# Two units of two neighbouring blocks beside each other in TensorE, 64 rows each, and the second layer's sums by channels

## The chip, the cores and the metric

One core of a Trainium2 chip runs the whole program. The metric is the device time of one execution in microseconds (us), the median of several. The kernel before takes 1239.06 us (median of 3 runs, 1237.01 to 1239.71).

## The reference, cut to what matters

```python
# x: (2, 4096, 192), weight: (8, 7); 8 heads of 24 channels
w = softmax(weight, axis=-1)
y[b, s, h, g] = sum_k w[h, k] * x_pad[b, s + k, h, g]     # causal, 7 taps
y = y.reshape(8192, 192)
h = y @ w_in                                              # 192 -> 2048
g = max(h, clip((h + 1) / 2, 0, 1) ** 2)                  # what the first layer's gate comes to
z = g @ w_out                                             # 2048 -> 192
h = z @ w_in2
out = (s * max(h, 0) ** 2 + b) @ w_out2                   # (8192, 192) float32
```

All inputs and outputs are float32. The second layer's `s` and `b` are scalars, so the kernel takes them out of the sum: out = s * (max(h, 0)^2 @ w_out2) + b * (column sums of w_out2).

## The kernel before, in words

**Tiles.** The 8192 tokens are 16 blocks of 512 (`NB`). The 2048 inner channels are 16 tiles of 128 (`f`). A unit is one layer, one block, one `f`: 512 units. Every product is made of several in a rounded format: an operand is split into a high part and a low part (`hA`, `lA`, `gh`, `gl`), and high x high, high x low and low x high are summed in PSUM.

**A unit.** `p1` (line 926) makes `h`, 128 inner channels by 512 tokens, of five matmuls with 512 columns: three for the first 128 of the 192 input channels (A), two for the last 64 (B). For B the high part of the weights stands in one half of the array's 128 rows, the low part in the other, and the moving tile holds the 64 channels twice, so that one pass makes two of the products. Then ScalarE and VectorE work on `h`: first layer a clip on ScalarE (line 975), a square (982), a maximum with `h` on VectorE (988); second layer a Relu (996) and a square (1003); in both the rounding to `gh` (967) on ScalarE and the rest `gl` (1010) on VectorE. The second product adds into PSUM banks over all 16 `f`. In the first layer it stands by channels: `pA` takes three matmuls (1022 to 1024) and `pB` two (1027, 1028), 512 columns each. In the second layer it stands by tokens: `gh` and `gl` are the weights, and for each of four groups of 128 tokens 384 columns of `w_out2` (high and low part) run against `gh` (1043) and 192 against `gl` (1044).

**After the last `f`.** In the first layer `evac_first` copies `pA` and adds the two halves of `pB` (1070, 1078, 1085). In the second layer `evac_second` scales on ScalarE (1136) and VectorE (1145), adds the bias on GpSimd (1159), and SyncE stores 96 KB for each 128 tokens.

**Banks.** PSUM has eight banks: four for `h` (`NH`), four for sums (`a`). A first-layer block uses two of the four, a second-layer block all four.

**Order.** Six stages: 6 blocks of layer one, 5 of layer two, and so on (`PHASES`); the first two blocks run in turns, unit by unit, and a third joins them. `Plan` is a list scheduler: each operation has a priority, a cost and the engines that it may run on, and the planner writes down one fixed order for each engine. Tiles come from pools ("f" and "o" are 512 columns wide), and an operation waits in the plan until a tile is free. The convolution of blocks 0 to 3 is done with matmuls (lines 845 and 872); that of the others on VectorE (698 to 725), while units of other blocks run. The weights arrive in 17 pieces, each split into high and low parts by five ScalarE and ten VectorE operations or so (544 to 650). At the start, `spread` (line 454) makes 16 small float32 matmuls, each of them two instructions with 32 rows: four products for each of the four groups of 32 rows, every group with a PSUM bank of its own.

## Time and profile before

| | |
|---|---|
| median of 3 runs | 1239.06 us |
| the profiled execution | 1239.57 us |
| its span, first to last instruction | 1237.9 us |
| TensorE matmuls busy | 1222.7 us (99%), 6096 instructions |
| TensorE weight loads busy | 1039.3 us (84%) |
| ScalarE busy | 1011.3 us (82%), 1791 instructions |
| VectorE busy | 757.3 us (61%), 1235 instructions |
| GpSimd busy | 49.6 us (4%), 86 instructions |
| mean granted clock of TensorE | 0.995 |

PE is TensorE's matmul row, PEld its weight loads, which run beside matmuls; DVE is VectorE, ACT ScalarE, POOL GpSimd, SP SyncE. The duration of a matmul in the trace is longer than the time until the next one starts, since matmuls follow each other in a pipeline; rates are read from starts.

### The profile page before, as it was taken

How to read it: one execution, taken by the hardware profiler on the slowest of the kernel's cores; microseconds unless marked ns; L12 is line 12 of the kernel's file. 1: busy time of each engine (PE TensorE's matmuls, PEld its weight loads, DVE VectorE, ACT ScalarE, POOL GpSimd, SP SyncE). 2: the span in 40 equal slices, each digit the busy share in tenths (PEclk: the TensorE clock that was granted, in tenths of full speed). 3: DMA queues.
4: the chain of work that ended last, by engine and by line, in shares of the span. 5: the costliest groups of instructions: out<-in, count | busy, mean ns of one | idle time of the engine just before them, and what ended most of it. 6: DMA issues, size and time to landing. Idle time of an engine off the chain costs nothing.

```text
span 1237.9 us, 16698 instructions
## 1 busy us (share of the span) xinstructions
PE 1222.7 (99%) x6096; PEld 1039.3 (84%) x6096; DVE 757.3 (61%) x1235; ACT 1011.3 (82%) x1791; POOL 49.6 (4%) x86
## 2 busy tenths in 40 slices
PE   7999999999999999999999999999999999999998
PEld 7877777879988987887888988888888888988887
DVE  5998999983333558695753333766875653333432
ACT  5898889987888888787788888887777778888886
POOL 1000000000000100000000000100000000000000
PEclk8999999999999999999999999999999999999999
DMA  5251312210001101100000001010100000000000
GB/s 134 68 111 26 73 31 60 45 26 5 19 22 31 31 14 27 19 18 10 9 9 4 19 22 40 22 34 16 26 1 1 9 9 3 20 22 23 22 14 13
DMA packets 67849, 34.24 MB, mean 28 GB/s; under 512 B 43197, under 2 KB 64183, under 8 KB 67767
## 3 DMA queue, kind: packets, MB, share of 16 engines
q1 hardware_dynamic: 67415, 32.94, 11.4%
q8 instruction: 47, 0.77, 0.3%
q14 instruction: 35, 0.29, 0.1%
q10 hardware_dynamic: 352, 0.25, 0.1%
HBM read 19.53 MB, written 6.29 MB: 21 GB/s over the span
## 4 chain that ended last, share of the span: by engine, by line
PE 82%; DVE 9%; ACT 6%; issue 1%; DMA 1%; POOL 0%; SPq 0%; POOLq 0%; DVEq 0%; ACTq 0%
PE h L926 41%; PE a L1043 16%; PE a L1044 7%; PE a L1024 4%; PE a L1027 3%; PE a L1028 3%; PE a L1023 3%; PE a L1022 3%; DVE o L1010 2%; DVE f L988 2%; DVE f L725 2%; ACT o L967 2%; ACT f L982 1%; ACT f L975 1%; PE h L845 1%
## 5 line engine op out<-in xcount | busy, mean ns | idle before, releaser
L1010 DVE TENSOR_TENSOR o<-f,o 128x512 fp32r<-128x512 f32 x512 | 357.4, 700 | 419.6 <-ACT o L967 417.0
L926 PE MATMUL h<-o,w 128*128 128x512 f32 x1536 | 445.5, 398 | 0.8 <-ACT o L750 0.6
L967 ACT CAST o<-f 128x512 fp32r<-128x512 f32 x509 | 313.9, 619 | 61.7 <-DVE f L988 52.3
L926 PE MATMUL h<-o,wB 128*128 128x512 f32 x1024 | 320.9, 394 | 0.0
L1043 PE MATMUL a<-w,o 128*128 128x384 f32 x1024 | 308.6, 357 | 0.7 <-DVE f L1085 0.7
L926 PEld LDWEIGHTS h<-o,w 128*128 128x128 f32 x1536 | 269.0, 188 | 46.4 <-ACT o L750 0.8
L1044 PE MATMUL a<-w,o 128*128 128x192 f32 x1024 | 257.2, 251 | 0.3 <-DVE o L1010 0.3
L926 PEld LDWEIGHTS h<-o,wB 128*128 128x128 f32 x1024 | 192.3, 188 | 45.7 <-DVE o L790 0.5
L996 ACT ACTIVATE f<-h 128x512 f32<-128x512 f32 x256 | 153.2, 598 | 76.0 <-PE h L926 75.3
L1043 PEld LDWEIGHTS a<-w,o 128*128 128x128 f32 x1024 | 192.2, 188 | 16.9 <-DVE y L1145 4.6
L1044 PEld LDWEIGHTS a<-w,o 128*128 128x128 f32 x1024 | 194.8, 190 | 10.6 <-DVE o L1010 0.5
L975 ACT ACTIVATE f<-h 128x512 f32<-128x512 f32 x256 | 152.0, 594 | 51.0 <-PE h L926 49.5
L988 DVE TENSOR_TENSOR f<-f,h 128x512 f32<-128x512 f32 x256 | 173.0, 682 | 23.0 <-ACT f L982 22.5
L1003 ACT ACTIVATE f<-f 128x512 f32<-128x512 f32 x256 | 161.8, 632 | 8.1
L982 ACT ACTIVATE f<-f 128x512 f32<-128x512 f32 x256 | 162.0, 633 | 4.5
L1024 PE MATMUL a<-o,w 128*128 128x512 f32 x256 | 103.1, 403 | 2.3 <-DVE o L1010 2.1
L1022 PE MATMUL a<-o,w 128*128 128x512 f32 x256 | 102.1, 399 | 0.2 <-ACT o L967 0.2
L1023 PE MATMUL a<-o,w 128*128 128x512 f32 x256 | 101.3, 396 | 0.0
L1027 PE MATMUL a<-o,w 128*128 128x512 f32 x256 | 100.9, 394 | 0.0
L1028 PE MATMUL a<-o,w 128*128 128x512 f32 x256 | 100.9, 394 | 0.0
L1159 POOL TENSOR_TENSOR y<-y,bias 128x192 f32<-128x192 f32 x64 | 44.5, 727 | 1182.7 <-DVE y L1145 881.1
L1024 PEld LDWEIGHTS a<-o,w 128*128 128x128 f32 x256 | 48.2, 188 | 21.4 <-DVE o L1010 10.2
(86 smaller groups left out, 664.0 us busy)
## 6 DMA issues: line engine op xcount, KB each, us to landing
f<-f SPq DMA_DIRECT2D x56, 128.0 KB
out_dram<-y SPq DMA_DIRECT2D x64, 96.0 KB
raw<-in_moe_w_out_dram SPq DMA_DIRECT2D x15, 384.0 KB
f<-in_x_dram SPq DMA_DIRECT2D x66, 68.0 KB
raw<-in_moe_w_in_dram SPq DMA_DIRECT2D x15, 256.0 KB
raw<-in_moe_w_in_dram SPq DMA_DIRECT2D x18, 128.0 KB
x<-in_x_dram SPq DMA_DIRECT2D x13, 120.0 KB
raw<-in_moe_w_out_dram SPq DMA_DIRECT2D x2, 192.0 KB
```

What stands on the lines that cost most here:

```text
L926: nc.tensor.matmul(h.ap, v, m.ap, start=(k == 0), stop=(k == len(terms) - 1))
L967: nc.scalar.copy(gh.ap, R())
L975: lambda _: nc.scalar.activation(R(), h.ap, IDENTITY_SAT15_5, scale=15.5),
L982: lambda _: nc.scalar.activation(R(), R(), AF.Square, bias=0.5, scale=1.0 / 31.0),
L988: lambda _: nc.vector.tensor_tensor(R(), R(), h.ap, op=ALU.max),
L996: lambda _: nc.scalar.activation(R(), h.ap, AF.Relu),
L1003: lambda _: nc.scalar.activation(R(), R(), AF.Square),
L1010: lambda _: nc.vector.tensor_tensor(gl.ap, R(), gh.ap.bitcast(F32), op=ALU.subtract),
L1022: nc.tensor.matmul(pA.ap, cols(P), gh.ap, start=first, stop=False)
L1024: nc.tensor.matmul(pA.ap, cols(P), gl.ap, start=False, stop=last)
L1043: nc.tensor.matmul(to, gh.ap[:, c], v, start=first, stop=False)
L1044: nc.tensor.matmul(to[:, 0], gl.ap[:, c], v[:, 0], start=False, stop=last)
```

## The change

- Two units run in one step: one of an even block and one of the odd block next to it, which is one `f` behind (`LAG`). So one of the two always has an even `f`, the other an odd one.
- The matmuls of a step have 64 rows each. One unit's matmul stands in rows 0 to 63 of the array, the other unit's in rows 64 to 127, each with its own weights, its own moving rows and its own PSUM bank. The B part of `p1` is three matmuls with 64 rows, with no doubled weights; of each matmul over 128 channels every unit does one half of the rows, and the other half later, when the two units have changed sides. `p1` is six pairs of matmuls and then three, the second product five pairs and then five.
- Before a unit adds into its bank from the other half of the rows, the earlier half must be through: `through` has GpSimd clear one element after the last matmul of the first part, and the first matmul of the second part waits for that.
- The first two steps and the last ones still use 128 rows (`full`, `full2`).
- The second layer's second product stands by channels, as in the first layer: `pA` with three terms and `pB` with two, 512 columns. `evac_second` scales and adds the bias by channels, VectorE transposes in 32x32 blocks, and the output is stored in pieces of 32 channels (`put_blocks`); the last two blocks are turned by TensorE and stored in rows (`put_rows`).
- The stages are 6, 4, 4, 6, 6, 6 blocks. The operands of a block are made five steps ahead (`GATE`). There are 26 "o" tiles in place of 19, 11 "f" tiles in place of 16, and the three "x" tiles become six "f" tiles once the first convolutions are done (`heirs`). A weight piece does two ScalarE casts and one VectorE add fewer.

```diff
-NX = 3
-XKEY = ((0, 2), (1.5, 2), (32.2, 1))
-PHASES = (6, 5, 5, 5, 5, 6)
-NRAW, NZ, NW, NFB, NOB, NY, NXW = 2, 1, 1, 16, 19, 4, 3
+PHASES = (6, 4, 4, 6, 6, 6)
+LAG = 1
+GATE = 5
+NFULL = 2
+NRAW, NZ, NW, NFB, NOB, NXW = 2, 1, 1, 11, 26, 3
...
-    units = sorted(
-        ((0, j, f) for j in range(NX) for f in range(NF)),
-        key=lambda t: XKEY[t[1]][0] + XKEY[t[1]][1] * t[2],
...
+    rows = [], []
+    done = [0, 0]
+        for j in range(done[l], done[l] + n):
+            rows[j % 2].extend((l, j, f) for f in range(NF))
...
+    steps = len(rows[0]) + LAG
+    step_of = {t: 2 * (k + LAG * q) + q for q in range(2) for k, t in enumerate(rows[q])}
...
+            pl.op(
+                need - 2.5,
+                dve1(P),
+                lambda _: nc.vector.tensor_tensor(
+                    tB.ap[:, P : 2 * P], wb.ap[:, colB:cols], zb.ap[:, colB:cols], op=ALU.add
+                ),
...
+    def units(k):
+        us = []
+        for q in range(2):
+            n = k - LAG * q
+            if 0 <= n < len(rows[q]):
+                us.append((2 * k + q, *rows[q][n], Buf("h"), Buf("o"), Buf("o")))
+        u0, full = us[0][0], k < NFULL or len(us) < 2
+        full2 = full or k >= len(rows[0]) - 2
+        us.sort(key=lambda t: t[3] % 2)
+        halves = [((UP, DN)[t[3] % 2]) for t in us]
+        hs = [t[4] for t in us]
+        def termsA(t):
+            (_, l, j, f, *_), op = t, operands[t[1], t[2]]
+            i, o = at[l, f]
+            w = lambda c: wF[l, i].ap[:, o, c : c + P]
+            return ((w(0), op["hA"]), (w(0), op["lA"]), (w(LOW), op["hA"]))
+        def termsB(t):
+            (_, l, j, f, *_), op = t, operands[t[1], t[2]]
+            w = wB[l, f // 2].ap
+            return ((w[:, 0:P], op["Bh"]), (w[:, 0:P], op["Bl"]), (w[:, P : 2 * P], op["Bh"]))
...
+        def through(u, bank):
+            def go(_):
+                i = nc.gpsimd.memset(seen.ap, 0.0)
+                tc.add_manual_dep(i.ins, lasts[bank], sync, reason="last of the one half")
+                lasts[bank] = i.ins.name
+            pl.op(u, ("pool", 100.0), go, reads=(bank,), parts=(seen,))
+        def side_by_side(terms, hv, start, stop):
+            follows = not start and lasts.get(hs[-1])
+            for n, ks in enumerate(zip(*terms)):
+                for (w, m), r, h in list(zip(ks, hv, hs))[:: 1 if start else -1]:
+                    i = nc.tensor.matmul(
+                        h.ap,
+                        w[r],
+                        m.ap[r],
+                        start=start and n == 0,
+                        stop=stop and n == len(terms[0]) - 1,
+                    )
+                    if follows:
+                        tc.add_manual_dep(i.ins, follows, sync, reason="first of the other half")
+                        follows = None
+            lasts[h] = i.ins.name
+        kw = dict(reads=[b for t in us for b in reads(t)], writes=hs)
+        if full:
+            def p1(_):
+                for t, h in zip(us, hs):
+                    for n, (w, m) in enumerate(termsA(t)):
+                        nc.tensor.matmul(h.ap, w, m.ap, start=n == 0, stop=False)
+                side_by_side([termsB(t) for t in us], halves, False, True)
+            cost = (3 * len(us) + 3) * SLOT + DRAIN
+            p1_ops.append(pl.op(u0, ("pe", cost), p1, after=p1_ops[-1:], **kw))
+        else:
+            def p1(_):
+                side_by_side([termsB(t) + termsA(t) for t in us], halves, True, False)
+            def p1_rest(_):
+                side_by_side([termsA(t) for t in us], halves[::-1], False, True)
+            p1_ops.append(pl.op(u0, ("pe", 6 * SLOT), p1, after=p1_ops[-1:], **kw))
+            through(u0, hs[1])
+            pl.op(u0 + 0.1, ("pe", 3 * SLOT), p1_rest, **kw)
+        for u, l, j, f, h, gh, gl in us:
+            between(u, l, h, gh, gl)
...
+            i, o = at[l, f]
+            if f == 0:
+                acc[l, j] = Buf("a"), Buf("a")
+            pA, pB = acc[l, j]
+            w = lambda c: wF[l, i].ap[:, o, c : c + P]
+            return (
+                (pA, lambda: w(P), gh, 0),
+                (pA, lambda: w(ROW - P), gh, 1),
+                (pA, lambda: w(P), gl, 2),
+                (pB, lambda: w(2 * P), gh, 0),
+                (pB, lambda: w(2 * P), gl, 2),
+            )
...
+        def p2(e, hv, start, stop):
+            follows = not start and lasts.get(terms[-1][3][0])
+            for n in (0, 1, 2, 3, 4) if start else (3, 4, 0, 1, 2):
+                for ts, (first, last), r in list(zip(terms, ends, hv))[:: 1 if start else -1]:
+                    p, w, m, at_n = ts[n]
+                    i = nc.tensor.matmul(
+                        p.ap,
+                        w()[r],
+                        m.ap[r],
+                        start=first and start and at_n == 0,
+                        stop=last and stop and at_n == 2,
+                    )
+                    if follows:
+                        tc.add_manual_dep(i.ins, follows, sync, reason="first of the other half")
+                        follows = None
+            lasts[p] = i.ins.name
...
+        if full2:
+                u0 + 2.5,
+                ("pe", 5 * len(us) * SLOT),
+                lambda e: p2(e, [slice(0, P)] * len(us), True, True),
...
+        else:
+            hv = (UP, DN)
+            pl.op(u0 + 2.5, ("pe", 5 * SLOT), lambda e: p2(e, hv, True, False), **kw)
+            through(u0 + 2.5, terms[1][3][0])
+            pl.op(u0 + 2.6, ("pe", 5 * SLOT), lambda e: p2(e, hv[::-1], False, True), **kw)
...
+        got = pl.op(
+            act_ps(NB, 186.0),
+                yB.ap[me, 0:NB], pB.ap[ot], AF.Identity, bias=bias.ap[me, 1:2], scale=sb2.ap[me, 0:1]
...
+        got = pl.op(
+            u + 3.2,
+            dve1(NB, 61.0),
+                out=yB.ap[me, 0:NB],
+                in0=pB.ap[me],
+                scalar=sb2.ap[me, 0:1],
+                in1=yB.ap[me, 0:NB],
...
+        if j >= NBLK - 2:
+            put_rows(u, j, me, yA, yB, got)
+            return
+        put_blocks(u, yA, ((j, 0, 0, P),))
+        if q:
+            put_blocks(u, yB, ((j - 1, 0, P, DB), (j, DB, P, DB)))
+    def put_blocks(u, y, parts):
+        t = Buf("f")
+            ("dve", 635.0),
+            lambda _: nc.vector.transpose(out=t.ap[:, 0:NB], in_=y.ap[:, 0:NB]),
...
+        for j, p0, c0, n in parts:
+            to = out[j * NB : (j + 1) * NB, :].rearrange("(a i) d -> i a d", i=HALO)
+            for b in range(0, n, HALO):
+                dma(
+                    u + 6,
+                    lambda _, to=to, p=p0 + b, c=c0 + b: nc.sync.dma_start(
+                        out=to[:, :, c : c + HALO],
+                        in_=t.ap[p : p + HALO, 0:NB].rearrange("i (a k) -> i a k", k=HALO),
...
+    for k in range(steps):
+        for q in range(2):
+            n = k + GATE - LAG * q
+            if 0 <= n < len(rows[q]):
+                l, j, f = rows[q][n]
+                if f == 0 and (l, j) not in operands:
+                    if l == 0 and j < NPE:
+                        conv_pe(j, 2 * (k + GATE) - 5, p1_ops[-1:])
+                    for nm in "AB":
+                        split(l, nm, j, 2 * (k + GATE) - 3, p1_ops[-1:])
```

## Rows read from the trace of the kernel before

**Rows 1.** The page: busy us (share of the span) xinstructions, then the chain by engine.
```profile
PE 1222.7 (99%) x6096; PEld 1039.3 (84%) x6096; DVE 757.3 (61%) x1235; ACT 1011.3 (82%) x1791; POOL 49.6 (4%) x86
...
PE 82%; DVE 9%; ACT 6%; issue 1%; DMA 1%; POOL 0%; SPq 0%; POOLq 0%; DVEq 0%; ACTq 0%
```

**Rows 2.** Windows by stage: length, busy time (xinstructions) by engine, granted clock, DMA.
```profile
20.00:100.00 80.00, 75.44 (x353) 60.27 (x352) 76.02 (x138) 70.66 (x134) 0.00 (x0) 0.98 0.43 99
100.00:140.00 40.00, 39.82 (x177) 31.61 (x175) 35.63 (x57) 32.05 (x60) 0.00 (x0) 1.00 0.06 14
140.00:200.00 60.00, 58.83 (x246) 45.22 (x246) 57.04 (x98) 52.85 (x97) 0.00 (x0) 1.00 0.23 58
200.00:266.50 66.50, 66.23 (x285) 53.11 (x284) 64.34 (x108) 57.81 (x109) 0.00 (x0) 1.00 0.17 37
266.50:456.40 189.90, 189.21 (x1062) 170.34 (x1062) 81.36 (x130) 159.04 (x275) 12.12 (x19) 1.00 0.09 22
456.40:641.80 185.40, 185.24 (x796) 148.74 (x795) 140.00 (x220) 145.82 (x260) 2.44 (x4) 1.00 0.08 17
```

**Rows 3.** Timeline from 1149.66 us, second layer: start us, us, instruction.
```profile
1149.66 0.63 PE L926 MATMUL h<-o,wB 128*128 128x512 f32 x2
...
1151.96 0.62 PE L926 MATMUL h<-o,wB 128*128 128x512 f32 x2
```

**Rows 4.** Windows of line 454 alone: length, PE busy, PEld busy, clock, DMA.
```profile
11.30:12.15 0.85, 0.85 (x11) 0.85 (x10) 0.50 0.04 11
12.80:13.65 0.85, 0.85 (x6) 0.85 (x5) 0.50 0.00 0
```

**Rows 5.** Groups of instructions, shapes apart: VectorE and ScalarE on 512 columns, the weight pieces.
```profile
L1010 DVE TENSOR_TENSOR o<-f,o 128x512 fp32r<-128x512 f32 x512 | 357.4, 700 | 419.6 <-ACT o L967 417.0 <-PE h L926 0.5 <-PE a L1027 0.5
L967 ACT CAST o<-f 128x512 fp32r<-128x512 f32 x509 | 313.9, 619 | 61.7 <-DVE f L988 52.3 <-PE a L1028 0.4
L1003 ACT ACTIVATE f<-f 128x512 f32<-128x512 f32 x256 | 161.8, 632 | 8.1
L996 ACT ACTIVATE f<-h 128x512 f32<-128x512 f32 x256 | 153.2, 598 | 76.0 <-PE h L926 75.3 <-DMA f<-f 0.3
L1085 DVE TENSOR_TENSOR f<-f,a 64x512 f32<-64x512 f32 x16 | 10.9, 684 | 2.0 <-ACT f L1070 1.7
L1070 ACT COPY f<-a 64x512 f32<-64x512 f32 x16 | 9.3, 582 | 0.4
L698 DVE STREAM_TRANSPOSE f<-f 128x544 f32<-128x544 f32 x18 | 13.3, 739 | 0.0
L650 DVE TENSOR_TENSOR wB<-w,z 64x128 fp32r<-64x128 f32 x32 | 9.2, 286 | 0.8
L1099 PE MATMUL h<-w,ones 128*128 128x384 f32 x16 | 3.0, 338 | 0.0
```

**Rows 6.** Groups of the second layer's way out: busy, mean ns, idle before.
```profile
L1136 ACT ACTIVATE y<-a,sb 128x192 f32<-128x192 f32 x64 | 23.1, 419 | 1.2 <-PE a L1044 1.2
L1145 DVE SCALAR_TENSOR_TENSOR y<-a,sb,y 128x192 f32<-128x192 f32 x64 | 23.3, 410 | 15.0 <-ACT y L1136 15.0
```

**Rows 7.** Waits: us in total, times, longest.
```profile
PEld a L1043 <- DVE y L1145: 4.6, 21, 0.4
```

**Rows 8.** Line 680, GpSimd's memsets: duration ns min/median/max.
```profile
L680 POOL MEMSET f<- x2: 123/126/130, 423.0 to 424.3; 128x32 f32 x1, 64x32 f32 x1
```

**Rows 9.** Timelines: the first unit, and the end from the last `gl`.
```profile
20.11 0.96 PE L926 MATMUL h<-o,w 128*128 128x512 f32 x3
20.91 0.93 PE L926 MATMUL h<-o,wB 128*128 128x512 f32 x2
...
1230.87 0.69 DVE L1010 TENSOR_TENSOR o<-f,o 128x512 fp32r<-128x512 f32 x1 [1.61 <-ACT o L967]
1231.62 0.36 PE L1044 MATMUL a<-w,o 128*128 128x192 f32 x1 [0.26 <-DVE o L1010]
1232.58 0.25 PE L1044 MATMUL a<-w,o 128*128 128x192 f32 x1
```

More of the change, by code (lines that the diff above doesn't have):

```diff
@@ L44, in __init__ @@
         self.writers, self.readers = [], []
[L45 removed]
+        self.left, self.end = 0, 0.0
     @property
@@ L165, in run @@
                 if not b.left and b.pool:
-                    self.pools[b.to].append((b.end, b.slot))
+                    self.pools[b.pool].append((b.end, b.slot))
+            for name, (to, cut) in self.heirs.items():
+                if not wanted[name]:
+                    self.pools[to] += [(t, v) for t, ap in self.pools[name] for v in cut(ap)]
+                    self.pools[name] = []
             ready.remove(o)
@@ L275 @@
     sb2 = fixed("sb2", [P, 2])
-    bias = fixed("bias", [P, D])
+    bias = fixed("bias", [P, 2])
     taps = fixed("taps", [H, KT])
@@ new lines, in emit_bias @@
+        for c0, c1, o in ((P, D, D), (0, P, ROW - 2 * P)):
+            pl.op(
+                u + 2.7,
+                act_ps(D),
+                lambda _, c0=c0, c1=c1, o=o: nc.scalar.copy(
+                    row.ap[:, c0:c1], p.ap[:, o : o + c1 - c0]
+                ),
+                reads=(p,),
+                parts=(row,),
+            )
+        pl.op(
+            u + 2.8,
+            dve1(D),
+            lambda _: nc.vector.tensor_tensor(
+                row.ap[:, 0:D], row.ap[:, 0:D], p.ap[:, 0:D], op=ALU.add
+            ),
+            reads=(p,),
+            writes=(row,),
+        )
@@ new lines, in emit_bias @@
+        pl.op(
+            u + 2.8,
+            dve1(D),
+            lambda _: nc.vector.transpose(out=col.ap[:, 0:D], in_=row.ap[:, 0:D]),
+            reads=(row,),
+            writes=(col,),
+        )
+        for b in range(0, D + DB, HALO):
+            q, c = slice(b % P, b % P + HALO), b if b < D else b - DB
+            pl.op(
+                u + 2.9,
+                ("dve", 120.0),
+                lambda _, b=b, q=q, c=c: nc.vector.tensor_scalar(
+                    bias.ap[q, b // P : b // P + 1],
+                    col.ap[q, c : c + 1],
+                    sb2.ap[q, 1:2],
+                    None,
+                    op0=ALU.mult,
+                ),
+                reads=(col, sb2),
+                parts=(bias,),
+            )
@@ new lines, in put_rows, with turn, copy @@
+    def put_rows(u, j, me, yA, yB, got):
+        for t in range(TT):
+            p, y = Buf("h"), Buf("f")
+            c = slice(t * P, (t + 1) * P)
+            def turn(_, p=p, c=c):
+                nc.tensor.transpose(p.ap[:, 0:P], yA.ap[:, c], ident.ap)
+                nc.tensor.transpose(p.ap[:, P:D], yB.ap[me, c], ident.ap[me, me])
+            def copy(e, p=p, y=y):
+                if e == "act":
+                    nc.scalar.copy(y.ap[:, 0:D], p.ap[:, 0:D])
+                else:
+                    nc.vector.tensor_copy(y.ap[:, 0:D], p.ap[:, 0:D])
+            pl.op(
+                u + 5, ("pe", 500.0), turn, reads=(yA, ident), writes=(p,), parts=(yB,), after=(got,)
+            )
+            pl.op(u + 5, (act_ps(D), dve1(D)), copy, reads=(p,), writes=(y,))
+            to = out[j * NB + t * P : j * NB + (t + 1) * P, :]
+            dma(u + 6, lambda _, to=to, y=y: nc.sync.dma_start(out=to, in_=y.ap[:, 0:D]), reads=(y,))
```

295 lines of the change are left out of this document (98 added, 197 removed).

## The prediction

> **What bounds the kernel now.** I read the page's busy shares first: matmuls 99% of the span, ScalarE 82%, VectorE 61%; the chain of waits that ended last runs over TensorE for 82% [rows 1]. Second the windows by stage: from 266 us on TensorE is busy in all of the time at a granted clock of 1.00; only up to 266 us is another engine near its limit, VectorE with 76.0 of 80, 57.0 of 60 and 64.3 of 66.5 us [rows 2]. Third the starts of matmuls, since a busy row says nothing of a rate. In the first layer the 80 units between 456.4 and 641.8 us take 185.4 us [rows 2], 2.3175 us each; a unit is ten matmuls of 512 columns, so one takes 0.2318 us. In the second layer a unit's start at 1149.66 is followed by the next at 1151.96: 2.30 us [rows 3], of five such matmuls (1.16) and eight of 384 or 192 columns (1.14). So time goes with the number of matmul slots, and only fewer slots, or shorter ones, help.
>
> **The slots after.** A step does two units. p1 is nine pairs of half-height matmuls, the second product ten: 19 slots of 512 columns, in either layer. If a pair takes the slot of one matmul, 0.2318 us, a step takes 4.403 us. First layer: two units took 4.635, so 0.232 us less for each of 128 pairs, 29.7 us. Second layer: 4.60, so 0.197 us less, 25.2 us; there p1 saves half a slot a unit, and ten slots for the second product stand against 2 x 1.14 us, the same. Together 54.9 us.
>
> **Does a pair take one slot?** No two matmuls of 512 columns stand beside each other in this trace. The nearest row is line 454, matmuls of 32 rows in four different groups of rows. At the same granted clock of 0.50 it shows 11 matmuls and 10 weight loads in 0.85 us while two groups are in the queue, and 6 and 5 in the last 0.85 us, where only the last group can be left [rows 4]. So two groups of rows run their matmuls and their loads beside each other, the second for next to nothing. It matters for the loads too: 1039 us for 6096 [rows 1] is 0.17 each, and two in a row would not fit into a slot. From below: nothing, 0.2318 us. From above: 11 counted against twice 6 leaves room for 9%, 0.253 us; and these matmuls have 52 columns, so they don't show two full streams into PSUM. I take 0.2318, since the counts are as near to twice as whole numbers come.
> The Trainium skill ("TensorE: Matmul & The Clock Gate", Measured speedup vs the span model) says that packed tiles take one matmul's time and about 4 ns for each further tile, and lists 3.07 times for four tiles of 32 rows and 512 columns. The row above is nearer to full overlap than 3.07 of 4. By the 4 ns all 4867 slots together would be 19 us longer; by 3.07 of 4 a slot would be 0.302 us and the kernel slower by some 300 us.
>
> **What is lost again**, term by term:
> - The odd block is one step behind: 255 steps of 19 slots and two lone units of 11, 4867 slots in all, 3 more than 256 steps: 0.7 us. The bias sums are 16 matmuls of 512 columns, 3.7 us for 3.0 [rows 5]: 0.7 us.
> - Up to 266.5 us VectorE is busy 233.0 of 246.5 us [rows 2]. The change takes 15 adds of 0.286 us out of that [rows 5], 4 us, and would make the stage 48 x 0.232 = 11 us shorter: about 229 of 235 us, 97%. No stage before kept TensorE full with more, so I take off 4.5 of the 11 us (between 0, as windows before were at 95%, and all 11).
> - Turnover of the sum banks. Both units of a step hold two of the four banks, so a block's first second product needs the banks of the block that ended one step earlier. Their way out after the last matmul: the end of its pipeline beyond the slot (two matmuls span 0.63 us [rows 3], so one lasts 0.40, 0.17 past its slot), two ScalarE copies of 0.582, a VectorE add of 0.684 [rows 5], and three hops of 0.06 (from VectorE's end at 1231.56 to TensorE's start at 1231.62 [rows 9]): 2.2 us. What the plan can set over it is the three slots of p1's second part, 0.70 us, and p1's first six, 1.39, if a pair of h banks is free: then all is covered; else 1.5 us is bare. There are 30 turnovers (15 in each row of blocks). I take 0.5 us each, 15 us, nearer to covered since h has two pairs of banks. Before, the second layer turned over four banks at once and VectorE's way out cost 4.6 us in 21 waits [rows 7]; that goes. Net 10.4 us, between -4.6 and 40.
> - The first p1 needs the B operand too, which came 0.8 us after A [rows 9]: 0.8 us. The end: before, from the last gl at 1231.56 to the span's end 6.3 us. After it the last unit has five slots (1.16), then a scaling by ScalarE, its VectorE add, transposes by TensorE, a copy and a store: 1 us more.
> - Rests (array between 128 and 64 rows, a wait now and then): 1.5 us.
> Sum 19.6. Costs taken at nothing: **GpSimd's clear** between the parts. Its hop is 0.17 of matmul pipeline, 0.13 of memset [rows 8] and two hops of 0.06, 0.42 us; TensorE's queue behind it stands still meanwhile, weight loads too, but the planner charges 0.59 us for it and sets the other product's part between, at least three slots or 0.70 us. Without that cover 508 hops cost up to 213 us. GpSimd itself is idle: its 49.6 us [rows 1] were mostly the bias adds, which go. **The way out of layer two**: ScalarE has 4 x 0.419 and VectorE 4 x 0.410 us a block before [rows 6]; after, ScalarE has two passes of 512 columns (about 1.3, an estimate from 0.582 for a plain copy [rows 5]), VectorE an add and one and a half transposes of 0.739 [rows 5], 1.8: even, and beside TensorE. **ScalarE**: three passes a unit, 0.598 + 0.632 + 0.619 [rows 5] = 1.85, 3.7 us of a step of 4.40, 84%; with splits and ways out it was 159 of 190 us in the second layer [rows 2] and comes to 88%: it fits. **Stores**: 84 more finely cut DMAs on SP, in the shape in which x is loaded; the DMA share in these stages is 0.08 to 0.09 [rows 2], and only a "f" tile waits for them. If any of these covers goes, it shows as the rivals below.
> 54.9 - 19.6 = 35.3 us. The profiled execution took 1239.57 us, its span is 1237.9, so 1.7 lie around it; it stands 0.5 above the median of 1239.06. 1237.9 - 35.3 = 1202.6, and 1.7 make **1204 us**. Its own range is 1187 (only the lone units, the bias, the start and the end are lost) to 1216.
>
> **Rivals.**
> 1. The turnovers, or the pair-wise bursts on ScalarE, lie bare: 30 x 1.5 in place of 30 x 0.5 is 30 us more, 1234. For: all four sum banks are in use all the time, and a late pair delays two units. Against: TensorE was full in a layer that also used all four [rows 2]. It gives 1216 to 1240.
> 2. Slower: two streams of 512 columns hinder each other, at each matmul. The price is 4867 times the excess; from 0.239 us a slot (7 ns, 35/4867) the gain is gone, and at the 0.253 that rows 4 leave room for it is 102 us more, 1306. For: twice the reads and twice the writes into PSUM, which no row shows. Against: the doubled counts. By the skill's 4 ns for the second tile, in that same section, the time would be 1224, inside the range.
> 3. Slower too: the hops through GpSimd lie bare. From 84 of 508 (35/0.42) the gain is gone; all bare would be 1417. For: the order on TensorE is fixed by planned costs. Against: 0.59 planned for 0.42 worked out.
> 4. The pairs don't run beside each other at all: 4867 more slots, 2332. Rows 4 speak against it.
>
> **Chances.** Forecast 65%, rival 1 20% (of it 4% within 0.2% of before, the rest faster), rival 2 11%, rival 3 3%, rival 4 1%. A measurement of this kernel tells about 0.2%, 2.5 us, from no change. So faster 81%, same 4%, slower 15%. The range runs from 1187 to 1236: it takes in most of rival 1 and leaves out the 15% and a little of either case.
>
> **What would show it.** In the profile after: some 9,900 matmuls, most with 64 rows; starts in the same half of the array 0.232 us apart, and the other half's between them; a step every 4.40 us in both layers. If starts are 0.24 apart or more, rival 2 is right. Waits of matmuls for GpSimd of more than a few us in sum show rival 3; waits for lines of evac_first or evac_second near each sixteenth step, rival 1; VectorE near 98% up to 255 us with waits of TensorE for gl, the second term. The prediction is wrong if the time is outside the range, and its reason is wrong if the slot isn't within 1% of 0.232.

## The result

The kernel after takes 1228.32 us (median of 4 runs, 1227.08 to 1228.73), the one before 1239.19 on the same chip (1237.01 to 1239.71): ratio 0.9914, 95% interval 0.9897 to 0.9931. So it is faster, by 10.9 us where 35 were forecast. The time lies in the range, 24 us above the value. The profiled execution took 1228.57 us with a span of 1226.8 and a mean granted clock of 0.992.

The page of the kernel after: busy us (share of the span) xinstructions, the chain by engine, then two groups (the second product, GpSimd's clear). They answer to [rows 1, 8].

```profile
PE 1189.5 (97%) x9900; PEld 1073.1 (87%) x9900; DVE 753.0 (61%) x1206; ACT 1004.6 (82%) x1738; POOL 51.1 (4%) x528
...
PE 69%; ACT 16%; DVE 10%; issue 2%; DMA 2%; SPq 0%; DVEq 0%; POOL 0%; ACTq 0%; POOLq 0%
...
L1013 PE MATMUL a<-o,w 64*128 64x512 f32 (+1 forms) x5080 | 710.0, 393 | 3.4 <-ACT x L1131 2.1
...
L941 POOL MEMSET seen<- 1x1 f32 x506 | 46.1, 91 | 1157.3 <-PE a L1013 605.9
```

TensorE is busy in 97% where it was 99%, and ScalarE has 16% of the chain where it had 6%: matmuls now wait for something that they did not wait for.

**The step.** Timeline of TensorE's matmuls in the kernel after, second layer: start us, us, instruction. It answers to [rows 3].

```profile
600.46 0.86 PE L951 MATMUL h<-o,wB 64*128 64x512 f32 x6
601.15 0.86 PE L951 MATMUL h<-o,w 64*128 64x512 f32 x6
601.85 1.33 PE L1013 MATMUL a<-o,w 64*128 64x512 f32 x10
603.00 0.87 PE L951 MATMUL h<-o,w 64*128 64x512 f32 x6
603.70 1.33 PE L1013 MATMUL a<-o,w 64*128 64x512 f32 x10
604.86 0.64 PE L951 MATMUL h<-o,wB 64*128 64x512 f32 x4
```

From 600.46 to 604.86 is one step: 4.40 us for 38 matmuls in 19 slots, and six half-height matmuls start within 0.69 us, 0.231 us a pair. That is the forecast's 4.403 and 0.2318.

**The stretches between.** Windows of the kernel after: start:end, length, busy us (xinstructions) of PE, PEld, DVE, ACT and POOL, granted clock, DMA share, GB/s. They answer to [rows 2].

```profile
20.00:260.00 240.00, 226.35 (x1819) 191.85 (x1820) 219.90 (x375) 195.12 (x352) 8.65 (x90) 0.99 0.27 63
260.00:560.00 300.00, 295.67 (x2500) 270.77 (x2498) 190.03 (x301) 248.19 (x426) 12.01 (x133) 0.99 0.10 19
560.00:860.00 300.00, 294.54 (x2503) 265.97 (x2501) 154.27 (x236) 254.09 (x432) 11.97 (x133) 1.00 0.12 22
860.00:1160.00 300.00, 293.97 (x2484) 270.93 (x2482) 159.75 (x240) 248.61 (x426) 11.61 (x131) 0.99 0.07 14
...
352.90:356.20 3.30, 3.30 (x20) 2.53 (x18) 1.54 (x3) 3.21 (x6) 0.09 (x1) 0.50 0.77 120
356.40:359.70 3.30, 3.30 (x31) 3.25 (x29) 1.14 (x2) 2.97 (x6) 0.09 (x1) 1.00 0.07 11
```

300 us of full slots hold 300 / 0.116 = some 2590 half-height matmuls; the three later windows have 2484 to 2503, 3% to 4% fewer. The last two lines show one reason that a busy row hides: in both TensorE is busy all the time, and at the granted clock of 0.50 (the 1.2 GHz level) it starts 20 matmuls where it starts 31 at 1.00.

Counted from the starts of matmuls in the two traces, the time inside slots fell from 1183.1 to 1130.7 us, by 52.4 (52 to 54, by the length that is taken for a slot). The time outside slots rose by 41.3:

| outside slots, us | before | after | more | forecast |
|---|---|---|---|---|
| up to 300 us | 41.6 | 55.4 | 13.8 | 8.3 (VectorE's stage 4.5, start 0.8, three of the 15 changes of pairs 3.0) |
| 300 to 1200 us | 7.4 | 31.7 | 24.3 | 8.9 (twelve changes 12.0, less the 4.6 of [rows 7]; rests 1.5) |
| the end | 5.8 | 9.0 | 3.2 | 1.0 |

(The forecast's other 1.4 us, lone units and bias, are slots.) 52.4 less 41.3 is 11.1, the difference of the spans.

The pair of blocks changes 15 times. Counted over the first six steps of each new pair, less the slots in them, the three changes up to 300 us have 9.5 us outside slots and the twelve later ones 28.6. That is 38.1 us where the forecast had 30 x 0.5 = 15. All other terms of the table come to 3.2 us, net of what before lost, and 3.2 were forecast for them.

**A turnover.** Timeline of the kernel after around the end of a pair of blocks: start us, us, engine, instruction, [idle before <- what ended it].

```profile
349.50 0.09 POOL L941 MEMSET seen<- 1x1 f32 x1 [3.17 <-PE h L951]
349.64 0.97 PE L951 MATMUL h<-o,w 64*128 64x512 f32 x6 [0.27 <-POOL seen L941]
349.94 0.77 ACT L1214 ACTIVATE f<-a,bias,sb 128x512 f32<-128x512 f32 x1
350.45 0.39 PE L951 MATMUL h<-o,wB 64*128 64x512 f32 x1
350.74 0.77 ACT L1232 ACTIVATE x<-a,bias,sb 64x512 f32<-64x512 f32 x1
...
351.54 0.60 ACT L1087 ACTIVATE f<-h 128x512 f32<-128x512 f32 x1
...
352.19 1.08 PE L951 MATMUL h<-o,wB 64*128 64x512 f32 x5 [1.34 <-ACT f L1087]
```

Read it as a chain. The next second product needs the sum banks, so the planner set the two parts of `p1` next to each other, and the hop through GpSimd lies bare at 349.64 (0.27 us idle; 0.42 from start to start beyond the slot, and 0.10 more before the next pair of matmuls starts). Then the next `p1` waits 1.34 us at 352.19 for an `h` bank, which the Relu of line 1087 frees. That Relu stands in ScalarE's queue behind the two scaled passes of the way out, lines 1214 and 1232, 0.80 us each from start to start (they take the place of the passes of [rows 6]). Six of the twelve changes have such a wait for a Relu, 9.3 us together. At three of them (352.9, 1079.9 and 1155.0 us) the clock of 0.50 follows the wait, about 1.6 us more each; behind the waits at 643.5, 716.7 and 1005.9 us, as long, the clock stays at 1.00. Bare hops, waits for VectorE's maximum and, in the first layer, three waits of second products for their sum banks (0.6 to 0.8 us) make the rest. 28.6 us for twelve changes are 2.4 a pair, 1.2 a block.

**Up to 260 us.** Timeline of the kernel after, while weights are still being prepared.

```profile
48.50 0.28 DVE L639 TENSOR_TENSOR w<-w,wB 128x128 f32<-128x128 f32 x1
...
48.82 0.29 DVE L648 TENSOR_TENSOR wB<-w,z 128x128 fp32r<-128x128 f32 x1
...
49.63 1.88 DVE L1079 TENSOR_TENSOR f<-f,h 128x512 f32<-128x512 f32 x3
...
50.36 0.74 PE L951 MATMUL h<-o,wB 64*128 64x512 f32 x4 [1.50 <-DVE f L1079]
```

The maximum of line 1079 frees the `h` bank in the first layer; it stands behind weight pieces, and TensorE is idle for 1.50 us before `p1` goes on. Four such waits, 1.45 to 1.68 us beyond the slot each, lie between 37 and 72 us.

The waits of the kernel after: us in total, times, longest. They answer to [rows 7].

```profile
PEld h L951 <- DVE f L1079: 14.4, 16, 2.0
PEld h L951 <- POOL seen L941: 11.8, 16, 1.0
...
PEld h L951 <- ACT f L1087: 7.3, 4, 2.1
...
PEld h L951 <- ACT x L1087: 3.6, 2, 1.8
```

Of 506 hops 16 hold up weight loads of `p1`, and 5 more those of a second product; most of the rest is what frees an `h` bank.

### The profile page after: what moved, and what is told of

It reads as the page before. It is cut to its first block, busy times and chain, and to the rows that moved or that the text cites. A ratio compares the mean times of both kernels' runs of the same rounds, so it can differ in the third digit from the quotient of the medians.

```text
span 1226.8 us, 24976 instructions
## 1 busy us (share of the span) xinstructions
PE 1189.5 (97%) x9900; PEld 1073.1 (87%) x9900; DVE 753.0 (61%) x1206; ACT 1004.6 (82%) x1738; POOL 51.1 (4%) x528
## 4 chain that ended last, share of the span: by engine, by line
PE 69%; ACT 16%; DVE 10%; issue 2%; DMA 2%; SPq 0%; DVEq 0%; POOL 0%; ACTq 0%; POOLq 0%
PE a L1013 37%; PE h L951 31%; ACT o L1058 3%; DVE o L1101 2%; ACT f L1073 2%; ACT f L1066 2%; DVE f L1079 2%; ACT f L1094 2%; ACT f L1087 1%; DMA raw<-in_moe_w_in_dram 1%; DVE x L1079 1%; DVE f L720 1%; ACT x L1094 1%; ACT x L1087 1%; PE h L840 1%
## 5 line engine op out<-in xcount | busy, mean ns | idle before, releaser
L1013 PE MATMUL a<-o,w 64*128 64x512 f32 (+1 forms) x5080 | 710.0, 393 | 3.4 <-ACT x L1131 2.1
L1013 PEld LDWEIGHTS a<-o,w 64*128 64x128 f32 (+1 forms) x5080 | 567.5, 185 | 55.0 <-DVE o L1101 4.9
L951 PE MATMUL h<-o,w 64*128 64x512 f32 x3048 | 481.6, 393 | 4.9 <-POOL seen L941 4.9
L951 PEld LDWEIGHTS h<-o,w 64*128 64x128 f32 x3048 | 351.4, 185 | 39.0 <-POOL seen L941 11.8
L1101 DVE TENSOR_TENSOR o<-f,o 128x512 fp32r<-128x512 f32 x336 | 230.0, 689 | 239.0 <-ACT o L1058 231.9
L951 PE MATMUL h<-o,wB 64*128 64x512 f32 x1536 | 250.2, 396 | 18.0 <-DVE f L1079 7.5
L951 PEld LDWEIGHTS h<-o,wB 64*128 64x128 f32 x1536 | 176.2, 185 | 42.5 <-DVE f L1079 14.4
L1101 DVE TENSOR_TENSOR o<-x,o 128x512 fp32r<-128x512 f32 x176 | 121.0, 689 | 126.9 <-ACT o L1058 124.3
L1058 ACT CAST o<-x 128x512 fp32r<-128x512 f32 x176 | 108.5, 618 | 16.9 <-DVE x L1079 13.8
L1073 ACT ACTIVATE f<-f 128x512 f32<-128x512 f32 x172 | 108.8, 632 | 5.2
L1094 ACT ACTIVATE f<-f 128x512 f32<-128x512 f32 x164 | 103.7, 632 | 5.2
L1094 ACT ACTIVATE x<-x 128x512 f32<-128x512 f32 x92 | 58.2, 632 | 2.9
L1073 ACT ACTIVATE x<-x 128x512 f32<-128x512 f32 x84 | 53.2, 633 | 2.5
```

What stands on the lines that cost most here:

```text
L951: i = nc.tensor.matmul(h.ap, w[r], m.ap[r], start=start and n == 0, stop=stop and n == len(terms[0]) - 1,)
L1013: i = nc.tensor.matmul(p.ap, w()[r], m.ap[r], start=first and start and at_n == 0, stop=last and stop and at_n == 2,)
L1058: nc.scalar.copy(gh.ap, R())
L1073: lambda _: nc.scalar.activation(R(), R(), AF.Square, bias=0.5, scale=1.0 / 31.0),
L1094: lambda _: nc.scalar.activation(R(), R(), AF.Square),
L1101: lambda _: nc.vector.tensor_tensor(gl.ap, R(), gh.ap.bitcast(F32), op=ALU.subtract),
```

## The experiments

"After" is the changed kernel, 1228.3 us; every time is a median, ratios are against the kernel before on the same chip.

**1. A short way out.** The operations that empty the sum banks read 64 of 512 columns; DMAs fill the other columns from another tile, so the output is not the reference's.

```diff
+EV = 64
...
-            act_ps(NB),
-            lambda _: nc.scalar.copy(sA.ap[:, 0:NB], pA.ap),
+            act_ps(EV),
+            lambda _: nc.scalar.copy(sA.ap[:, 0:EV], pA.ap[:, 0:EV]),
...
```

> Of the changed kernel (1228.3 us) the operations that empty the sum banks after a block's last f read 64 columns in place of 512, and the plan knows it; the other columns of these tiles are filled from another tile by DMA, so the output is not the reference's. Theory (turnover): the loss beside the forecast sits where a pair of blocks ends. There the next second product waits for its sum banks, the two parts of p1 follow each other with a bare hop of 0.43 us, and the next p1 waits up to 1.5 us for an h bank, since ScalarE is emptying sums; after 260 us that is 25 us over 12 changes of a pair. With a way out of some 0.7 us in place of 2.2 it falls by half or more: 1203 to 1216 us. Rival (the hops, or VectorE with the weights): the turnover is not the place, less than 5 us gained, 1223 or more.

1205.34 us (1204.84 to 1205.58), ratio 0.9724 (0.9709 to 0.9738): 23 us less than after, inside the range expected. Its later windows are fuller than those of after:

```profile
260.00:560.00 300.00, 299.29 (x2556) 268.34 (x2554) 186.43 (x297) 248.85 (x438) 12.23 (x136) 1.00 0.14 31
...
860.00:1160.00 300.00, 298.75 (x2564) 271.28 (x2563) 147.14 (x227) 250.37 (x438) 11.92 (x135) 1.00 0.10 23
```

So the loss after 260 us hangs on the turnovers: the twelve changes have 8.9 us outside slots where after has 28.6 (the 25 of the expectation was a lower count of the same). Whether by the banks' latency or by what the passes push back on ScalarE, this run does not say.

**2. The first layer's maximum left out** (the operation of line 1079, and with it the `max` of the gate).

> The changed kernel without the first layer's maximum on VectorE (256 passes of 0.68 us; the output is not the reference's); h is then free after ScalarE's clip. Theory: up to 260 us VectorE is the limit: p1 waits for h banks that VectorE has not read yet, 1.5 to 1.7 us each time when a weight piece is split (four times between 37 and 70 us) and about 4.5 us around 181 to 201 us. These go, and some of the first layer's turnovers: 8 to 14 us faster, 1214 to 1220. Rival (only turnovers and hops cost, VectorE is hidden): less than 3 us.

1217.05 us (1212.9 to 1219.5), ratio 0.9815 (0.9787 to 0.9844), 11.3 less than after, as expected; two of its four runs, with a mean clock of 0.987 where the others have 0.994 and 0.995, took 1219.4 and 1219.5, so part of the gain is the clock. Up to 260 us VectorE is busy 182.17 of 240 us, TensorE 233.14 where it was 226.35:

```profile
20.00:260.00 240.00, 233.14 (x1900) 191.77 (x1901) 182.17 (x306) 210.49 (x365) 10.20 (x94) 1.00 0.27 63
```

So the first stage waits for VectorE's maximum in a good part: 6.8 of the 13.65 us that TensorE was idle there are gone. Whether by its place in the queue or by VectorE's load, this run does not say; experiment 12 does.

**3. A longer hop.**

```diff
                 i = nc.gpsimd.memset(seen.ap, 0.0)
+                for _ in range(2):
+                    i = nc.gpsimd.memset(seen.ap, 0.0)
```

> The changed kernel with three clears by GpSimd in place of one in each of the 506 hops, so each hop is about 0.2 us longer, 0.62 in place of 0.42, with the order of all engines unchanged. Theory: a hop lies under the other product's part (at least three slots, 0.70 us) but for some 20 at the turnovers, where it is bare: 20 x 0.2 = 4 us, 1230 to 1237. Rival (hops bare everywhere): 506 x 0.2 = 100 us, 1328.

1237.8 us (1235.77 to 1239.52), ratio 0.9988 (0.9978 to 0.9997): 9.5 more than after, just above the range expected and a tenth of the 100 of bare hops. From its list of waits (5 of these in after):

```profile
PEld a L1015 <- POOL seen L944: 30.4, 92, 1.0
```

92 hops now hold up weight loads of the second product that stood behind three slots of the other, but the matmuls mostly start in time. The cover that the forecast named is real, and has little to spare.

**4. Full height for all but B.** `NFULL = 2` becomes 1000, so only B's three slots of a step have 64 rows.

> One part alone: only the B part of p1 runs as two halves beside each other; its A part and the second product use all 128 rows, in all steps. The slots are the same 19 a step and no hop through GpSimd is left, but the array changes between 128 and 64 rows twice in each step. Theory: each change costs the pipeline's end, 0.1 to 0.2 us, 256 x 2 of them: 51 to 102 us slower, 1270 to 1330. Rival (a change of shape costs nothing): the bare hops go, some 8 us faster, 1220.

1280.1 us (1277.82 to 1281.92), ratio 1.0326 (1.0307 to 1.0346), 52 more than after. Its timeline shows a step:

```profile
601.65 1.54 PE L969 MATMUL h<-o,w 128*128 128x512 f32 x6
603.12 0.96 PE L951 MATMUL h<-o,wB 64*128 64x512 f32 x6
604.01 2.58 PE L1013 MATMUL a<-o,w 128*128 128x512 f32 x10
606.42 1.55 PE L969 MATMUL h<-o,w 128*128 128x512 f32 x6
```

Six full matmuls take 1.47 us where six slots are 1.39, three pairs 0.89 where three slots are 0.70, ten full ones 2.41 where ten are 2.32: 4.77 us from 601.65 to 606.42, 0.37 more than a step of after, for a change of height and back. Over 254 steps that would be 94 us. The 52 measured are net: TensorE, slower by itself, now waits for little (it is busy 299.3 to 300.0 of 300 us in the later windows), and the bare hops are gone too. The number of slots is that of after, so a step that mixes heights pays for each change, and one that stays at half height, as after does, pays none.

**5. ScalarE has one pass less in the second layer's way out.**

```diff
-            (act_ps(NB, 186.0), dve1(NB, 122.0)),
+            dve1(NB, 122.0),
```

> One edit to the changed kernel (1228.3 us): in evac_second the scaling of pA runs on VectorE (planned 0.72 us) and no longer on ScalarE (0.80 from start to start), beside ScalarE's pass over pB. Theory (turnover): in the second layer the way out shrinks from about 2.4 to 1.6 us and ScalarE comes 0.8 us earlier to the Relu that frees an h bank; the four waits of 1.5 us for it (350, 715, 1078, 1153 us) shrink to about 0.7, and the three stretches of half granted clock behind them, 1.5 us each, go: 5 to 10 us faster, 1218 to 1223. Rival (the first layer's turnovers and VectorE's load make the loss): within 2 us of 1228.

1218.43 us (1217.38 to 1220.68), ratio 0.9842 (0.9827 to 0.9857), 9.9 less than after, as expected. 0.80 us of work ahead of the Relu are gone, and `p1` still waits for a Relu at the same changes, 1.17 us idle at 351.64 where it was 1.34. But VectorE's pass now runs beside ScalarE's, so the banks come free sooner too: at the change shown above their last reader ends 4.5 us after the block's last second product in after, 3.1 us in this kernel. So the run does not tell ScalarE's queue from the banks' latency. 3.1 us of the gain are the clock, which between the first 40 us and the last slots falls to 0.50 once (at 194.9) and not three times. The bare hop ahead of the wait is gone at 351.64 too.

**6. The second layer's sums by channels alone**, in the kernel before, with full height and no pairs.

```diff
-        if l == 0:
-            if first:
-                acc[0, j] = Buf("a"), Buf("a")
-            pA, pB = acc[0, j]
+        if first:
+            acc[l, j] = Buf("a"), Buf("a")
+        pA, pB = acc[l, j]
...
```

> One part alone, put into the kernel before (1239.4 us): the second layer's second product and its way out by channels, with 128 rows, one unit after the other; p1 and the order are those of before. A unit goes from 2.30 to 2.3175 us in the second layer: 256 x 0.0175 = 4.5 us more, and 0.7 for the bias sums. A block then uses two of four sum banks, so the next block starts in the other two, and the waits of 5.5 us for VectorE's way out go. Theory (the turnover costs because both blocks of a pair hold all four banks): 1236 to 1242, no turnover waits in its trace. Rival (the way out by channels is slow in itself): waits at each of 15 block ends, 10 us or more slower than before, 1250.

1243.84 us (1243.39 to 1244.6), ratio 1.0046 (1.003 to 1.0063): 5.1 more than before, a little above the range expected. A second-layer unit now takes 2.3175 us for 2.30, 256 x 0.0175 = 4.5 us, and the bias sums 0.7 more. That these 5.2 are the whole difference is chance: from 1200 us on this kernel has 9.2 us outside slots where before has 5.8, and between 300 and 1200 us it has some 4 fewer. The only wait of second products that its list of waits shows is one for `gl`, 27 times and on the weight loads:

```profile
PEld a L1022 <- DVE o L1010: 10.6, 27, 1.0
```

Channels cost no turnover where a block has its own pair of banks to change to. The turnover comes with the pairs.

**7. The odd block three steps behind:** `LAG = 1` becomes 3.

> One number changed in the changed kernel: the odd block is three steps behind in place of one, so the two blocks of a pair end 13 us apart. Four more lone units cost 4 x 1.5 slots, 1.4 us. Theory: the turnover of one block still has no spare bank, but ScalarE no longer empties two blocks in a row; some of the loss goes, 3 to 8 us in all: 1221 to 1227. Rival (each turnover pays for itself alone): 1228 to 1231.

1218.28 us (1217.52 to 1220.38), ratio 0.9841 (0.9826 to 0.9856), 10 less than after, where 3 to 8 were expected. The two ways out are three steps apart, so the scaled passes of the pair no longer stand together; and the clock does not fall at any of them, which is 4.7 of the 10.

**8. Planned anew.** Several costs of the planner at once: ScalarE's latency (9, below), the pass of 5, the other scaled pass at 0.80 us, the hop through GpSimd 0.14 us less, operands and weights a little earlier.

```diff
-GATE = 5
+GATE = 7
-SECOND = (56, 94)
+SECOND = (60, 110)
-    WAIT = {"none": 0.0, "pe": 250.0, "act": 140.0, "dve": 130.0, "pool": 240.0, "sp": 0.0}
+    WAIT = {"none": 0.0, "pe": 250.0, "act": 140.0, "dve": 130.0, "pool": 100.0, "sp": 0.0}
...
-            act_ps(NB, 186.0),
+            act_ps(NB, 320.0),
```

> A version meant to be faster: the scaling of pA on VectorE as in the run beside it; the planner charges 0.13 us between a ScalarE operation and the ScalarE operation that needs its result (the traces show 0.626 from a Relu's start to its square's, where 0.48 was planned), 0.80 for the scaled pass over pB (0.66 planned) and 0.45 in place of 0.59 for a hop; operands are made seven steps ahead, and the second layer's weights are due from step 60 to 110 rather than 56 to 94. Theory: the turnover and VectorE's early stage make the loss, and both get smaller: 1208 to 1218. Rival (they are fixed by four banks and by VectorE's work): 1220 or more.

1192.65 us (1190.08 to 1194.04), ratio 0.9629 (0.9614 to 0.9645): 35.7 less than after, 46 less than before, and the fastest kernel here, well under the 1208 to 1218 expected. It does the same matmuls in another order. The next four take it apart.

**9. ScalarE's latency alone.** The planner let a ScalarE operation that reads the result of the one before start at once; it now charges 0.13 us.

```diff
-            same = d.at == eng and eng != "dve"
-            t = max(t, d.end + (0.0 if same else self.WAIT[d.at]))
+            same = d.at == eng and eng not in ("dve", "act")
+            w = 130.0 if d.at == eng == "act" else self.WAIT[d.at]
+            t = max(t, d.end + (0.0 if same else w))
```

> One of the edits of the 1192.7 us version alone, put into the changed kernel (1228.3 us): the planner charges 0.13 us between a ScalarE operation and the ScalarE operation that needs its result. No work changes, only the written order, since ScalarE in the plan of the changed kernel is faster than on the chip (Relu to square 0.626 us by the trace, 0.478 planned). Theory A (the order was written for a ScalarE that is too fast, so at turnovers it comes late to the h banks): this is the largest part, 12 to 18 us faster, 1210 to 1216. Rival B (the parts are alike and small): 3 to 8 us, 1220 to 1225.

1198.93 us (1198.79 to 1199.86), ratio 0.9678 (0.9664 to 0.9693): 29.4 less than after, where 12 to 18 were expected. First ScalarE's timeline in the kernel after, two units of the second layer:

```profile
621.72 0.60 ACT L1087 ACTIVATE x<-h 128x512 f32<-128x512 f32 x1 [0.67 <-PE h L951]
622.35 0.64 ACT L1094 ACTIVATE x<-x 128x512 f32<-128x512 f32 x1
623.02 0.62 ACT L1058 CAST o<-x 128x512 fp32r<-128x512 f32 x1
623.54 0.59 ACT L1087 ACTIVATE f<-h 128x512 f32<-128x512 f32 x1
```

then the same in this kernel, where the two units' passes stand in pairs:

```profile
609.79 1.09 ACT L1088 ACTIVATE f<-h 128x512 f32<-128x512 f32 x2 [1.26 <-PE h L952]
610.76 1.15 ACT L1095 ACTIVATE f<-f 128x512 f32<-128x512 f32 x2
611.80 1.14 ACT L1059 CAST o<-f 128x512 fp32r<-128x512 f32 x2
```

In the kernel after Relu, square and cast of one unit take 621.72 to 623.54 = 1.82 us; the code charges 0.478 + 0.520 + 0.520 = 1.52. Of its 256 Relus 255 are followed at once by their own square, and these starts are 0.626 us apart. Here 123 are followed by the other unit's Relu (0.494 us) and 123 by its square (0.478): the same work without the wait for a result. Windows of this kernel:

```profile
20.00:260.00 240.00, 230.13 (x1853) 197.04 (x1853) 223.92 (x392) 190.92 (x358) 10.54 (x91) 1.00 0.27 63
260.00:560.00 300.00, 298.66 (x2564) 271.86 (x2562) 186.75 (x297) 235.99 (x439) 12.19 (x137) 1.00 0.10 19
560.00:860.00 300.00, 298.67 (x2564) 277.51 (x2562) 163.11 (x259) 232.46 (x434) 12.11 (x134) 1.00 0.12 22
860.00:1160.00 300.00, 299.94 (x2588) 274.33 (x2586) 143.95 (x225) 234.10 (x437) 12.18 (x136) 1.00 0.07 14
```

ScalarE is busy 232 to 236 us of 300 for 248 to 254 in after, TensorE has its 2564 to 2588 matmuls, and the clock is 1.00. No matmul after 260 us waits for a Relu any more; some 0.42 us hops at turnovers are left. The twelve changes have 7.1 us outside slots where after has 28.6: the seven into a second-layer pair next to none, the five into a first-layer pair the 7. There are still four sum banks and the same passes empty them, so at these seven neither the banks nor the length of the way out made the loss; the order did. 4.7 us of the gain are the clock's three falls, which do not come here. The edit lets the passes of two units stand in pairs everywhere and sets those at a change elsewhere; no run separates these two.

**10 to 12. The other edits.** Kernel 8 without the edit of 9; the hop's planned cost alone (`"pool"` from 240 to 100); `GATE` and `SECOND` alone.

> The 1192.7 us version without that one edit; the scaling of pA on VectorE, the 0.80 and 0.45 us in the plan, seven steps and the later weights remain. Theory A: it loses the largest part again, 1205 to 1212. Rival B: 1196 to 1200.

> The changed kernel with one number of the plan changed: after a GpSimd operation others wait 0.10 us in the plan in place of 0.24, so a hop is planned with 0.45 us, near the 0.43 that bare hops show. Theory A: order around turnovers changes little, 0 to 4 us faster. Rival B: 4 to 8 us.

> The changed kernel with operands made seven steps ahead in place of five, and the second layer's weights due from step 60 to 110. Theory A: VectorE's rush around 181 to 201 us eases and the splits stand further from a turnover: 3 to 6 us faster, 1222 to 1225. Rival B: nothing, since VectorE's work is the same: 1227 to 1230.

1207.03 us (1206.79 to 1208.7), ratio 0.9745 (0.973 to 0.9759); 1221.93 (1220.07 to 1225.19), 0.9867 (0.9845 to 0.9889); 1220.47 (1219.95 to 1221.12), 0.9851 (0.9836 to 0.9865). So the last two are 6.4 and 7.9 us less than after (0 to 4 and 3 to 6 were expected), and 14.4 us of kernel 8's gain need the edit of 9. Singly, the edits of 5, 9, 11 and 12 give 9.9, 29.4, 6.4 and 7.9, in sum 53.6, together 35.7: they take the same waits away. Above all the same falls of the clock: in the profiled executions of 9 and 11 none of the three comes, in those of 5 and 12 there is one in the whole stretch, so that 3.1 to 4.7 us of each gain are the clock alone. Timeline of kernel 11 at the change shown above:

```profile
349.45 0.96 PE L951 MATMUL h<-o,w 64*128 64x512 f32 x6 [0.27 <-POOL seen L941]
...
352.00 0.95 PE L951 MATMUL h<-o,wB 64*128 64x512 f32 x5 [1.35 <-ACT x L1087]
...
353.27 1.55 PE L1013 MATMUL a<-o,w 64*128 64x512 f32 x10
```

The hop and the wait are those of after, but the next second product starts 1.27 us behind the wait, where in after it is 1.73 (352.19 to 353.92 us): here the clock did not fall. In kernel 12, up to 260 us, VectorE is busy 223.64 us (219.90 in after) and TensorE 230.42 (226.35): with no less work for VectorE, in another order, TensorE waits less.

**13. The same latency in the kernel before.** The edit of 9, nothing else.

> The kernel before, with nothing but the planner's cost of a dependent ScalarE operation changed: 130 ns between a ScalarE operation and the next that reads it, where it had 0. Theory A, the 29 us that this edit gave to the changed kernel are time that the change itself lost, since only there ScalarE's late passes leave TensorE without work: before, TensorE is busy in all of the time from 266 us on, so at most some of the 41.6 us that lie outside matmul slots up to 300 us can go: 1232 to 1240 us. Theory B, a better order is worth the same to either kernel, and the change's own worth stays at 11 us: 1208 to 1222 us.

1233.19 us (1231.23 to 1234.2), ratio 0.9955 (0.9942 to 0.9969): 5.8 less than before. In the profiled execution the last `p1` starts 6.3 us earlier than before. 3.6 of this are won by 260 us; the rest comes later, though TensorE looks busy there in both (300 us from 560 on hold 1540 matmuls, 1531 before), against the expectation that only the time up to 300 us has something to give:

```profile
20.00:260.00 240.00, 235.46 (x1041) 186.83 (x1040) 230.50 (x395) 208.24 (x391) 0.00 (x0) 0.99 0.25 60
...
560.00:860.00 300.00, 300.00 (x1540) 260.24 (x1539) 161.96 (x256) 244.65 (x431) 15.21 (x20) 1.00 0.09 19
```

So most of the 29.4 us are time that only the changed kernel had lost. With this one cost right in both, the change is worth 1233.2 - 1198.9 = 34.3 us. That 35 were forecast is luck: counted in the same way, this pair of kernels loses 11.1 us more up to 300 us, 5.6 then and 2.8 behind the last slot, for 8.3, 8.9 and 1.0.

## Why the prediction was right in sign and wrong in size

- **The slots: right.** 53.5 us net were forecast, 52.4 are counted (52 to 54). Two 512-column streams in two halves of the rows cost each other nothing that shows: 0.231 us a pair. That settles rivals 2 and 4. The 4 ns for a further tile, which the Trainium skill states ("TensorE: Matmul & The Clock Gate", Measured speedup vs the span model), do not show in a steady stream: the second of a pair starts some 4 to 18 ns after the first, but six matmuls start within 0.69 us, three slots.
- **The turnovers: the step that failed**, "I take 0.5 us each, 15 us, nearer to covered since h has two pairs of banks". Measured: 1.27 us each, 38.1 for the 15. The other terms are right in sum (3.2 for 3.2), so the 24 us that the time lies above the value are this term's 23 and 1 of the slots. The way out was worked out at 2.2 us to the banks' release, and the cover as slots of `p1`, "if a pair of h banks is free". That condition was taken as nearly met because there are two pairs; when the next pair comes free was not worked out. In the second layer ScalarE's Relus free them, and at six changes they stood behind the passes of the same way out (five times the scaled passes, once the copies of the first layer). It is rival 1 in place and kind, the bursts on ScalarE included; its price lay between the forecast's and its own 1.5. The time is inside the range only because the range took in most of rival 1.
- **"ScalarE ... it fits": true of the mean, false of the queue.** 84% was forecast for the unit passes, and ScalarE is busy 248 to 254 of 300 us. The prediction's own sum for a unit, 1.85 us, was right (1.82 by the starts); what was not asked is what the plan charges for it. Rows of before could have told: of its 256 Relus 253 are followed at once by their square, 0.631 us after their start, where the code charges 0.478. Before, TensorE stayed full all the same from 266 us on [rows 2]; after, two units come at once, their chains stand one behind the other, and a late one stops 19 slots. Experiments 9 and 13 show it: 29.4 us there, 5.8 here, for the same edit (4.7 of the 29.4 are the clock). The Trainium skill ("ScalarE: Activation LUTs", What ACT_TABLE_LOAD costs) says that ACTIVATEs back to back overlap by about 93 ns. The trace agrees roughly for independent ones (a Relu is 0.595 us long and the next pass starts 0.478 to 0.494 after it, an overlap of 0.10 to 0.12); dependent ones do not overlap (0.626 apart).
- **The clock: not in any term.** Three stretches at 0.50 behind turnover waits cost some 1.6 us each, 4.7 of the 28.6. Of the other versions only experiment 3's has more than one such fall in its profiled execution, so that of the gains over after 3.1 to 4.7 us are the clock, whatever the edit.
- **VectorE's stage: near in size, wrong in its reason.** Up to 300 us 13.8 us are lost for 8.3, but 9.5 lie at three changes of pairs. From 20 us on and apart from these, after has 26.9 us outside slots, before 21.6 in all: some 5 for the 4.5 of this term. The two can't be parted cleanly, since at these changes `p1` waits for VectorE's maximum as well. The share was forecast at 97%; it is 219.90 of 240, 92%. It was not a full VectorE but the order in its queue: the maximum stands behind weight pieces (the timeline at 48 us, experiments 2 and 12).
- **The end: 3.2 for 1.0.** "A scaling by ScalarE, its VectorE add, transposes by TensorE, a copy and a store" was named but not worked out; experiment 6, without pairs, loses as much at its end, so it is the price of the way out by channels. The timeline of after (it answers to [rows 9]) has the last sum's matmul before 1218.95, 0.46 us of waiting for the add and sixteen transposes to 1223.18:

```profile
1218.95 0.27 PE L1289 MATMUL h<-ident,f 128*128 128x128 f32 x1
1219.69 0.27 PE L1290 MATMUL h<-ident,f 64*128 64x64 f32 x1 [0.46 <-DVE f L1241]
...
1222.91 0.27 PE L1290 MATMUL h<-ident,f 64*128 64x64 f32 x1
```

- **The hops: right.** 0.42 us was worked out, and a bare one costs 0.42 to 0.43. Rival 3 is out: 21 of 506 hold up weight loads, mostly at turnovers (those of `p1` 11.8 us in the list of waits, and 4.9 of matmuls).

Open: what of experiment 8's last 6.3 us over 9 belongs to which edit; how much of experiment 9's 29.4 us any other shift of the order would have given, since all four single edits of the order (5, 7, 11, 12) gave 6 to 10; why the first stage still has 5.8 us (of 240) without a matmul in the best order (experiment 8); and why the clock falls behind some of these waits and not behind others as long.

## What to carry to other kernels

When a change makes the bounding engine's work shorter, the other engines' queues get the same work in less time. Go through each queue at the places where a rare job (emptying a bank, preparing weights) joins the regular one, and ask for the next buffer that the bounding engine needs, not only for the one that the rare job holds. In an order written by planned costs, compare the cost with starts, not durations, in the trace, dependent pairs apart; an error that a full engine hides today is paid once its work shrinks.

## What the runs showed of the hardware

- Two streams of matmuls with 64 rows each and 512 columns, in different halves of the array, run at 0.231 us a pair, the time of one full-height matmul (0.232), their weight loads with them.
- Going from full height to half and back costs about 0.37 us a step (experiment 4).
- After a wait the second pair of matmuls starts 0.33 us behind the first, not 0.23 (349.64 and 349.98 us in after).
- A ScalarE pass of 512 columns that reads the result of the one before starts 0.626 us after it behind a Relu, 0.664 behind a square; an independent one 0.478 to 0.494 and 0.520. A pass with scale and bias from a tile takes 0.80 from start to start.
- Behind a bare hop and a wait of 1.3 us at a turnover the granted clock fell to 0.50 (the 1.2 GHz level) three times in after, and a pair of matmuls then started every 0.43 us. It stayed at 1.00 behind the same hop and wait twice in after and five times in kernel 11.
